# Pace of the second MoE's first weights, precedence of its first input sums, and place of the rests' last output products

## The chip, the core and the metric

The kernel runs on one core of one Trainium2 chip. The metric is device time in microseconds, median of the runs. A profiled execution has a span (first to last instruction) and a time of its own, which is a little longer than the span.

## What is computed

Nyström attention, then a gated MLP (SiLU gate, called layer 1 here) and a second one (sigmoid gate, layer 2), on 4 batches of 576 tokens.

```python
A, Bm, C = sm(q, k_lm), sm(q_lm, k_lm), sm(q_lm, k)      # 32 landmarks
Z = pinv_by_6_iterations(Bm)
x = (A @ Z @ C @ v)                                      # (2304, 512)
g = x @ w_gate;  x = (g * sigmoid(g) * (x @ w_val)) @ w_out      # layer 1, d_ff 1536
gate = sigmoid(x @ w_gate2);  out = (gate * (x @ w_val2)) @ w_out2   # layer 2
```

## The kernel before

All matrices are split into a high and a low fp32r part, and a product is three matmuls (high·high, low·high, high·low). The MLP weights arrive as 64-bit floats. `convert` turns a raw tile into fp32 with two ScalarE instructions (L329, L332) and two VectorE instructions (L334, L338); `split` makes the high part by a ScalarE cast (L365) and the low part by a VectorE subtraction (L366).

**Layer 1** goes over six chunks `c` of 256 hidden columns and four batches `b`. A string of words sets the order: `U` makes the chunk's folded weights `uw`, `G` the gate and value products (`pg`, `pv`), the gate function on ScalarE (L528, tile `sg`), its product with the value on VectorE (L529, tile `h`) and the split of `h`; `O` makes the output products `po`, added to `acc` on VectorE (L583). So `G50` is chunk 5, batch 0. The first 64 tokens of each batch are gathered into a block of 256 tokens, the *rests*, which is batch number 4 in `O` words and in layer 2. Between the steps of a word, `emit` takes `nw` steps out of `wfill`, the list of weights that are still to be prepared. From the word after `G43` on, the first weights of layer 2 (`weights(1, 0)`) are in that list. Whatever is left when layer 2 begins is done at once by `need(1, 0, 3)` at L834.

**Layer 2** runs in two passes: `st` 1 for batches 0 and 1 and the rests, `st` 2 for batches 2 and 3. A pass treats its input as 2 x 2 blocks and makes seven block products instead of eight. `x_blocks` prepares it for each half `j` of the inner dimension: four sums `xs` (L615 to L618), and for seven blocks a high part in `AH` and a low part `xl` (L366). `pair_steps` issues the block products (`pg`, `pv` with the chunk and the product number in their names), `rest_steps` the rests' (`pgr`, `pvr`), and `o2_steps` the output products of the chunk before, added to `oacc` (L750) and, after the last chunk, written out by four DMAs a tile on SyncE's queue (L756). The argument `ths` of `o2_steps` is the order: 0 and 1 are the two batches of the pass (four tiles of 128 tokens each), 2 the rests (two tiles).

Buffers come from pools with a set number of slots. The two `oacc` tiles of the rests live in the pool `xs`, and so do the sums `xs` and some low parts `xl` of both passes: an `xl` of the second pass takes the slot of a rests' tile when that has been written out. PSUM has three slots for `gv`, two each for `o` and `a`, and one for `n`; every fourth gate or value product of layer 1, and the value of product 2 in layer 2, takes the slot `n`.

The instructions of an engine run in the order in which a scheduler put them, by the program's order and its priorities (`tc.high_priority(n)` moves work forward by `n`). Each engine and each DMA queue is in order.

Of the kernel before, what the change touches and what calls it, by code (L numbers as in the profile page):

```python
# [16 lines left out]
def nystrom_moe_kernel(tc, q, k, v, wg1, wv1, wo1, wg2, wv2, wo2, out):  # L17
# [11 lines left out]
    NFC = DFF // FC  # L29
# [4 lines left out]
    def pool(name, side=None, **kw):  # L34
        return tc.alloc_tile_pool(name=name, bufs=1, side=side, reuse_waits="tile", **kw)
# [10 lines left out]
    def ptile(shape, tag, name):  # L46
        return psum.tile(shape, F32, tag=tag, name=name, bufs=PB[tag])

    late = {}
# [14 lines left out]
    def mm(o, l, r, start=True, stop=True):  # L64
        return nc.tensor.matmul(o, l, r, start=start, stop=stop, skip_group_check=True)  # L65
# [27 lines left out]
    def step(fill, n=1):  # L93
        while n and fill:
            try:
                next(fill[0])
                n -= 1
            except StopIteration:
                fill.pop(0)
# [264 lines left out]
    def split(hi, lo, x):  # L364
        nc.scalar.copy(hi, x)  # L365
        nc.vector.tensor_tensor(lo, x, hi.bitcast(F32), op=ALU.subtract)  # L366
# [60 lines left out]
    def weights(layer, c):  # L427
        if layer == 0:
            W1[c] = w1p.tile([P, 4, 2, FC], F32, tag="w1", name=f"w1_{c}", bufs=2)
            wo_tile(layer, c)  # L430
            i0 = PIECES.index((layer, c, load_in, 0))
            for j in range(4):
                load_to(i0 + j + 3)
                yield from convert(loaded[i0 + j], W1[c][:, j])
        else:
            wo_tile(layer, c)
            for j in range(2):
                yield from in_weights(layer, c, j)
        ready.add((layer, c, 3))
        for j in range(2):  # L440
            yield from out_weights(layer, c, j)
        ready.add((layer, c, 5))
        load_to(PIECES.index((layer, c, load_out, 1)) + 4)
# [8 lines left out]
    def need(layer, c, part):  # L452
        while (layer, c, part) not in ready:
            step(wfill)
# [11 lines left out]
    def otag(layer, c):  # L466
        nps[0] += 1
        return "oa"[nps[0] % 2] if layer or c >= OA else "o"
# [4 lines left out]
    ACC = {}  # L473
# [68 lines left out]
    NR = S - MT  # L542
# [61 lines left out]
    def x_blocks(step_, x):  # L604


        hi = [AH[:, s, NR:] for s in range(16)]
        for j in range(2):
            def new(n, dt, home):
                pool_, bufs = (per, 16) if home == "CL" else (late["xs"], 8)  # L610
                return pool_.tile([P, MT], dt, tag=home, name=f"x{n}{step_}_{j}", bufs=bufs)

            a11, a12, a21, a22 = x[0][j], x[0][2 + j], x[1][j], x[1][2 + j]
            s1, s2, s3, s4 = (new(f"s{n}", F32, "xs") for n in range(1, 5))
            nc.vector.tensor_tensor(s1, a21, a22, op=ALU.add)  # L615
            nc.vector.tensor_tensor(s3, a11, a21, op=ALU.subtract)
            nc.vector.tensor_tensor(s2, s1, a11, op=ALU.subtract)
            nc.vector.tensor_tensor(s4, a12, s2, op=ALU.subtract)  # L618
            for n, at, src, home in ((1, 0, a11, "CL"), (2, 8, a12, "CL"), (4, 9, a22, "CL"), (5, 2, s1, "CL"),
                                     (6, 10, s2, "xs"), (7, 1, s3, "xs"), (3, 3, s4, "xs")):  # L620
                lo = new(f"l{n}", F32R, home)
                split(hi[at + 4 * j], lo, src)
                XB[n, j] = (hi[at + 4 * j], lo)
# [107 lines left out]
    def o2_steps(step_, c, ths):  # L731
        w = WO[step_, c]
        for th in ths:
            h = [H2[ft, th] for ft in range(2)]
            i = th + 2 * step_ - 2 if th < 2 else B
            for t in range(0, MT if i < B else NR * B, P):
                if c == 0:
                    OACC[i, t] = (per.tile([P, DM], F32, tag="CL", name=f"oacc{i}_{t}", bufs=16) if i < B else
                                  late["xs"].tile([P, DM], F32, tag="xs", name=f"oacc{i}_{t}", bufs=8))
                acc = OACC[i, t]  # L740
                ps = ptile([P, DM], otag(1, c), f"po2_{c}_{i}_{t}")
                n = 0
                for ft in range(2):
                    for a, x in TERMS:
                        mm(ps, h[ft][a][:, t:t + P], w[:, x, ft, :], start=(n == 0), stop=(n == 5))
                        n += 1
                if c == 0:
                    nc.scalar.copy(acc, ps)
                else:
                    nc.vector.tensor_tensor(acc, ps, acc, op=ALU.add)  # L750
                if c == NFC - 1:
                    rows = out.rearrange("(b t u) d -> b u t d", b=B, u=L)
                    for y in range(P // M):
                        bb, u = (i, (NR + t) // M + y) if i < B else ((t + M * y) // NR, (t + M * y) % NR // M)
                        eng = nc.scalar if y % 2 and step_ == 2 else nc.sync
                        eng.dma_start(rows[bb, u], acc[M * y:M * y + M, :])  # L756
                yield
# [19 lines left out]
    def emit(word, nw=1):  # L777
        gens = [iter(KINDS[t[0]](*map(int, t[1:]))) for t in word.split("+")]
        fill = word[0] in "UPGO"
        while gens:  # L780
            for g in list(gens):
                try:
                    next(g)
                except StopIteration:
                    gens.remove(g)
            if fill:
                step(wfill, nw)
# [18 lines left out]
    for word in words.split():  # L806
        kind, c, bs = word[0], int(word[1]), [int(b) for b in word[2:]]
        if kind == "G" and bs == [1] and c < NFC - 1:
            wfill.append(weights(0, c + 1))
        if kind == "O":  # L810
            need(0, c, 5)
        elif kind != "G":
            need(0, c + bs[-1] // B, 3)
        emit(word, 2)
        if word == f"G{NFC - 2}3":
            late["uw"].release()
            late["w2"] = pool("w2")
            late["x"] = pool("x")
            wfill.append(weights(1, 0))
    w1p.release()  # L820
    late["xs"] = pool("xs")
    x_blocks(1, [[ACC[b, dm][:, NR:] for dm in range(4)] for b in range(2)])

    def run(g, n=100, nw=2):
        for _ in range(n):
            try:
                next(g)
            except StopIteration:
                return
            step(wfill, nw)  # L830
# [11 lines left out]
    prev = None  # L842
    for st in (1, 2):
        for c in range(NFC):
            if st == 1 or c + 1 < NFC:
                wfill.append(weights(st, c + 1) if c + 1 < NFC else weights(2, 0))
            rest = rest_steps(c) if st == 1 else iter(())
            o2 = iter(())
            if prev:
                need(*prev, 5)  # L850
                o2 = o2_steps(*prev, (0, 1) if prev[0] == 2 else (0, 1, 2) if prev[1] == NFC - 1 else (2, 0, 1))
            if (st, c) == (1, NFC - 1):
                x2 = [[per.tile([P, MT], F32, tag="CL", name=f"x2{b}_{dm}", bufs=16) for dm in range(4)]
                      for b in range(2)]
                for dm in (0, 2, 1, 3):
                    for b in range(2):
                        nc.sync.dma_start(x2[b][dm], XP[b + 2, dm])
            if (st, c) == (2, 0):
                x_blocks(2, x2)
            run(o2, 10 if (st, c) == (2, 0) else 4 if st == 2 else 6)  # L860
            need(st, c, 3)
            if c < NFC - 1:
                run(rest)
            if prev:
                g2 = pair_steps(st, c)
                run(g2, 5)
            for n in (4, 2, 4):
                run(o2, 1)
                run(g2, n)
            run(o2)  # L870
            run(g2)
            run(rest)
            prev = (st, c)
# [39 lines left out]
```

## Time and profile before

| | |
|---|---|
| median of 3 runs | 884.43 us (882.47 to 886.38) |
| profiled execution, own time | 883.13 us |
| its span | 881.3 us |
| PE busy | 843.0 us, 96% of the span |
| VectorE (DVE) busy | 662.4 us, 75% |
| ScalarE (ACT) busy | 475.2 us, 54% |
| mean granted TensorE clock | 0.988 of full speed |

TensorE (PE) is busy nearly all the time, so what can be had lies in the few places where it stands still, and in the work that runs at the lower of its two clock levels (1.2 in place of 2.4 GHz) after it. Busy shares are read by stage: another engine may be full in a stage in which its average is low.

### The profile page before, as it was taken

How to read it: one execution, taken by the hardware profiler on the slowest of the kernel's cores; microseconds unless marked ns; L12 is line 12 of the kernel's file. 1: busy time of each engine (PE TensorE's matmuls, PEld its weight loads, DVE VectorE, ACT ScalarE, POOL GpSimd, SP SyncE). 2: the span in 40 equal slices, each digit the busy share in tenths (PEclk: the TensorE clock that was granted, in tenths of full speed). 3: DMA queues.
4: the chain of work that ended last, by engine and by line, in shares of the span. 5: the costliest groups of instructions: out<-in, count | busy, mean ns of one | idle time of the engine just before them, and what ended most of it. 6: DMA issues, size and time to landing. Idle time of an engine off the chain costs nothing.

```text
span 881.3 us, 15891 instructions
## 1 busy us (share of the span) xinstructions
PE 843.0 (96%) x6172; PEld 698.7 (79%) x6172; DVE 662.4 (75%) x1295; ACT 475.2 (54%) x967; POOL 57.7 (7%) x90
## 2 busy tenths in 40 slices
PE   5698999999999999997999999999999899999998
PEld 4386778888889888887878888888888778888886
DVE  4989776776886776689698667879789965687655
ACT  5787556355653443357347655555646465455431
POOL 4634330000000000000000000000000000000000
PEclk9899999999999999998999999999999989999999
DMA  8876211032430211036204315344255442242003
GB/s 267 211 218 201 81 56 29 3 96 69 124 96 18 68 60 49 1 143 208 79 34 158 120 45 195 97 143 167 97 179 170 123 134 89 95 120 71 1 25 96
DMA packets 41483, 93.31 MB, mean 106 GB/s; under 512 B 5824, under 2 KB 8896, under 8 KB 41408
## 3 DMA queue, kind: packets, MB, share of 16 engines
q1 hardware_dynamic: 40640, 91.25, 33.2%
q10 hardware_dynamic: 768, 1.05, 0.5%
q8 instruction: 48, 0.79, 0.4%
q14 instruction: 27, 0.22, 0.1%
HBM read 72.88 MB, written 19.40 MB: 105 GB/s over the span
## 4 chain that ended last, share of the span: by engine, by line
PE 83%; DVE 9%; ACT 3%; DMA 3%; issue 1%; SPq 1%; POOL 0%; ACTq 0%; DVEq 0%; POOLq 0%
PE po L65 31%; PE pg L65 20%; PE pv L65 20%; PE pu L65 2%; DMA raw<-in_moe_w_val_dram 2%; PE pgr L65 2%; PE pvr L65 2%; PE tp L148 1%; PE nw L65 1%; DVE cv L334 1%; PE cs L65 1%; DVE xl L366 1%; PE as L65 1%; DVE acc L583 1%; ACT cv L329 1%
## 5 line engine op out<-in xcount | busy, mean ns | idle before, releaser
L65 PE MATMUL po<-wo,h 128*128 128x512 f32 x432 | 109.5, 390 | 0.0
L65 PE MATMUL po<-h,wo 128*128 128x512 f32 (+1 forms) x480 | 105.4, 374 | 0.3 <-DVE uw L366 0.2
L65 PEld LDWEIGHTS po<-h,wo 128*128 128x128 f32 x480 | 83.4, 190 | 27.3 <-issue 7.5
L65 PE MATMUL pv<-AH,uw 128*128 128x288 f32 x552 | 93.3, 300 | 5.7 <-ACT sg L528 5.2
L65 PE MATMUL pg<-AH,uw 128*128 128x288 f32 x552 | 95.6, 300 | 1.3 <-ACT uw L365 1.0
L65 PEld LDWEIGHTS po<-wo,h 128*128 128x128 f32 x432 | 80.7, 188 | 17.6
L65 PEld LDWEIGHTS pv<-AH,uw 128*128 128x128 f32 x552 | 80.2, 191 | 10.1 <-ACT sg L528 6.1
L65 PEld LDWEIGHTS pg<-AH,uw 128*128 128x128 f32 x552 | 80.8, 189 | 6.5 <-issue 2.5
L750 DVE TENSOR_TENSOR oacc<-po,oacc 128x512 f32<-128x512 f32 x90 | 60.2, 685 | 31.5 <-PE po L65 31.4
L329 ACT ACTIVATE cv<-raw 128x512 f32<-128x512 f32 x84 | 56.7, 676 | 35.5 <-DVE st L338 8.8
L65 PE MATMUL pg<-AH,wt 128*128 128x512 f32 x192 | 60.8, 398 | 2.0 <-DVE wt L425 2.0
L65 PE MATMUL pv<-AH,wt 128*128 128x512 f32 x192 | 60.5, 396 | 0.0
L65 PE MATMUL po<-hh,wo 128*128 128x288 f32 x256 | 58.9, 310 | 0.0
L334 DVE SCALAR_TENSOR_TENSOR cv<-cv,cv 128x512 uint32<-128x512 uint32 x84 | 57.8, 692 | 0.8 <-ACT cv L332 0.8
L332 ACT ACTIVATE cv<-raw 128x512 uint32<-128x512 uint32 x84 | 56.1, 672 | 4.2 <-DVE wo L366 4.1
L583 DVE TENSOR_TENSOR acc<-po,acc 128x512 f32<-128x512 f32 x64 | 43.6, 687 | 18.2 <-PE po L65 17.9
L528 ACT ACTIVATE sg<-pg 128x288 f32<-128x288 f32 x64 | 26.0, 406 | 45.7 <-PE pg L65 45.6
L365 ACT CAST h<-h 128x288 fp32r<-128x288 f32 x64 | 27.5, 433 | 34.1 <-DVE h L529 34.1
L65 PEld LDWEIGHTS po<-hh,wo 128*128 128x128 f32 x256 | 41.6, 188 | 4.8 <-issue 2.4
L65 PEld LDWEIGHTS pg<-AH,wt 128*128 128x128 f32 x192 | 36.6, 191 | 10.3 <-DVE wt L425 2.4
L65 PE MATMUL pv<-AH,wk 128*128 128x512 f32 x144 | 44.3, 389 | 0.0
L65 PE MATMUL pg<-AH,wk 128*128 128x512 f32 x144 | 44.1, 390 | 0.0
(196 smaller groups left out, 1741.0 us busy)
## 6 DMA issues: line engine op xcount, KB each, us to landing
raw<-in_moe_w_out_dram SPq DMA_DIRECT2D x36, 512.0 KB, 4.3
raw<-in_moe_w_gate_dram SPq DMA_DIRECT2D x48, 128.0 KB, 2.9
raw<-in_moe_w_val_dram SPq DMA_DIRECT2D x48, 128.0 KB, 2.9
raw<-in_moe_w_gate_dram SPq DMA_DIRECT2D x24, 256.0 KB, 3.0
raw<-in_moe_w_val_dram SPq DMA_DIRECT2D x24, 256.0 KB, 3.7
wkd<-st SPq DMA_DIRECT2D x24, 256.0 KB, 3.2
wtd<-tf SPq DMA_DIRECT2D x12, 512.0 KB, 3.5
st<-wkd SPq DMA_DIRECT2D x24, 256.0 KB, 2.9
```

The lines of the kernel that those rows point to most:

```text
L65: return nc.tensor.matmul(o, l, r, start=start, stop=stop, skip_group_check=True)
L148: nc.tensor.transpose(ps[:, j], flat(src[:, 2 * u:2 * u + 2]), ident)
L329: nc.scalar.activation(t0, hiw.bitcast(F32), AF.Copy, scale=2.0 ** -112)
L332: nc.scalar.activation(u1, low, AF.Copy, scale=0.875 * 2.0 ** -29, bias=0.49)
L334: nc.vector.scalar_tensor_tensor(u1, u0, 3, u1, op0=ALU.logical_shift_left, op1=ALU.bitwise_or)
L365: nc.scalar.copy(hi, x)
L366: nc.vector.tensor_tensor(lo, x, hi.bitcast(F32), op=ALU.subtract)
L528: nc.scalar.activation(sg, pss[0], AF.Silu)
L583: nc.vector.tensor_tensor(sl, ps, sl, op=ALU.add)
L750: nc.vector.tensor_tensor(acc, ps, acc, op=ALU.add)
```

## The change

Three edits, none of which adds or removes an instruction.

```diff
@@ layer 1's words
-        emit(word, 2)
+        emit(word, 1 if late.get("w2") else 2)
         if word == f"G{NFC - 2}3":
             late["uw"].release()
             late["w2"] = pool("w2")
...
     late["xs"] = pool("xs")
-    x_blocks(1, [[ACC[b, dm][:, NR:] for dm in range(4)] for b in range(2)])
+    with tc.high_priority(300):
+        x_blocks(1, [[ACC[b, dm][:, NR:] for dm in range(4)] for b in range(2)])
...
-                o2 = o2_steps(*prev, (0, 1) if prev[0] == 2 else (0, 1, 2) if prev[1] == NFC - 1 else (2, 0, 1))
+                o2 = o2_steps(*prev, (0, 1) if prev[0] == 2 else (0, 2, 1) if prev[1] == NFC - 1 else (2, 0, 1))
```

The first takes one step of layer 2's first weights where two were taken, in the words after `G43`. The second gives the sums and splits of the first pass precedence. The third puts the rests' last output products between those of batch 0 and batch 1 when the second pass begins.

**First place: ScalarE at `G50`.** Before, between the first two gates (`sg_5_0`; `cv`, `wk`, `wo` and `wt` are weights):

```order
L424 CAST wt_0_0_5546<-tf_0_0_5496 128x1024
L365 CAST wk_0_01_5577<-st_0_1_5557 128x512
L329 ACTIVATE cv_5625<-raw 128x512
L332 ACTIVATE cv_5626<-raw 128x512
L528 ACTIVATE sg_5_0_5680<-pg_5_0_5666 128x288
L365 CAST wk_0_11_5602<-st_0_1_5557 128x512
L329 ACTIVATE cv_5660<-raw 128x512
L332 ACTIVATE cv_5661<-raw 128x512
L365 CAST wo_0_5494<-cv_5626 128x512
L329 ACTIVATE cv_6354<-raw 128x512
L332 ACTIVATE cv_6355<-raw 128x512
L528 ACTIVATE sg_5_0_5705<-pg_5_0_5691 128x288
```

And now, at the same place:

```order
L329 ACTIVATE cv_5670<-raw 128x512
L332 ACTIVATE cv_5671<-raw 128x512
L424 CAST wt_0_0_5586<-tf_0_0_5496 128x1024
L528 ACTIVATE sg_5_0_5637<-pg_5_0_5623 128x288
L528 ACTIVATE sg_5_0_5662<-pg_5_0_5648 128x288
L365 CAST h<-h_5_0_5638 128x288
L365 CAST wk_0_01_5645<-st_0_1_5601 128x512
L528 ACTIVATE sg_5_0_5688<-pg_5_0_5674 128x288
L365 CAST h<-h_5_0_5663 128x288
L329 ACTIVATE cv_5748<-raw 128x512
L528 ACTIVATE sg_5_0_5709<-pg_5_0_5695 128x288
```

Six weight instructions stood between the first gate and the second; now the two are neighbours, and the weights stand between the gates of `G50`, `G51` and `G52`. VectorE's weights move in the same way.

**Second place: VectorE and TensorE at the start of layer 2.** `h_5_3_6127` is the last of layer 1's four products of `G53`, `xs` and `xl` the first pass's sums and low parts. VectorE, as a piece of the difference:

```order
 L366 TENSOR_TENSOR h<-h_5_3_6107,h 128x288
-L529 TENSOR_TENSOR h_5_3_6127<-sg_5_3_6126,pv_5_3_6119 128x288
 L615 TENSOR_TENSOR xs_0_6136<-acc_0_2339,acc_2_2357 128x512
-L366 TENSOR_TENSOR h<-h_5_3_6127,h 128x288
 L616 TENSOR_TENSOR xs_0_6138<-acc_0_1131,acc_0_2339 128x512
 L617 TENSOR_TENSOR xs_0_6137<-xs_0_6136,acc_0_1131 128x512
...
 L366 TENSOR_TENSOR xl_1_6188<-xs_1_6167,AH 128x512
 L366 TENSOR_TENSOR xl_1_6191<-xs_1_6168,AH 128x512
+L529 TENSOR_TENSOR h_5_3_6127<-sg_5_3_6126,pv_5_3_6119 128x288
+L366 TENSOR_TENSOR h<-h_5_3_6127,h 128x288
```

`h_5_3_6127` and its low part stood before and behind the first of the sums; now all 19 instructions of `x_blocks` from L615 `xs_0_6136` to L366 `xl_1_6191` go first. TensorE after the change, from the first value product of layer 2 on:

```order
L65 MATMUL pv_1_0_1_6212<-AH,wk_0_01_5645 128x512 x2
L65 MATMUL po_5_3_6236<-h,wo_5_5090 128x512 x3
L65 MATMUL po_5_3_6246<-h,wo_5_5090 128x512 x3
L65 MATMUL po_5_3_6256<-h,wo_5_5090 128x512 x3
L65 MATMUL po_5_3_6266<-h,wo_5_5090 128x512 x3
L65 MATMUL pg_1_0_1_6198<-xl_1_6173,wk_0_01_5645 128x512
L65 MATMUL pv_1_0_1_6212<-xl_1_6173,wk_0_01_5645 128x512
L65 MATMUL pg_1_0_2_6205<-xl_1_6176,wk_0_11_5718 128x512
L65 MATMUL pv_1_0_2_6219<-AH,wk_0_10_5554 128x512 x2
L65 MATMUL pv_1_0_2_6219<-xl_0_6147,wk_0_10_5554 128x512
L65 MATMUL pv_1_0_2_6219<-AH,wk_0_11_5718 128x512 x2
L65 MATMUL pv_1_0_2_6219<-xl_1_6176,wk_0_11_5718 128x512
```

Before, the five matmuls of `pv_1_0_2` that need no `xl_1` stood directly behind `pv_1_0_1`, and the products `po_5_3` came whole; now `po_5_3` comes in halves, and `pv_1_0_2` comes behind the first halves. It takes the PSUM slot `n` of `pv_5_3_6119`, which is free when the moved L529 has read it.

**Third place: SyncE's queue at the start of the second pass.** `oacc_0_6556` and `oacc_128_6573` are the rests' tiles, the other `oacc` those of batches 0 and 1.

```order
 L756 DMA out_dram<-oacc_384_6637 32x512 x4
+L756 DMA out_dram<-oacc_0_6556 32x512 x4
+L756 DMA out_dram<-oacc_128_6573 32x512 x4
 L756 DMA out_dram<-oacc_0_6800 32x512 x4
 L756 DMA out_dram<-oacc_128_6860 32x512 x4
 L756 DMA out_dram<-oacc_256_6887 32x512 x4
-L756 DMA out_dram<-oacc_384_6927 32x512 x4
-L756 DMA out_dram<-oacc_0_6556 32x512 x4
-L756 DMA out_dram<-oacc_128_6573 32x512 x4
+L756 DMA out_dram<-oacc_384_6927 32x512 x3
+L414 DMA tf_1_1_8475<-wtd_1_6518 128x1024
+L756 DMA out_dram<-oacc_384_6927 32x512
```

The rests' output DMAs move from the 33rd to 40th place among the forty to the 17th to 24th, and a weight load (`tf_1_1`) now stands ahead of the last output DMA and of the weight loads behind it. On VectorE the rests' additions (L750) move forward by the same four tiles.

## Rows read from the trace of the kernel before

**Rows 1.** Page, parts 1 and 4: busy us by engine; chain that ended last

```profile
PE 843.0 (96%) x6172; PEld 698.7 (79%) x6172; DVE 662.4 (75%) x1295; ACT 475.2 (54%) x967; POOL 57.7 (7%) x90
...
PE 83%; DVE 9%; ACT 3%; DMA 3%; issue 1%; SPq 1%; POOL 0%; ACTq 0%; DVEq 0%; POOLq 0%
```

**Rows 2.** Stretches: width, then busy us of each engine, clock, DMA

```profile
core 0: us, PE busy (x) PEld busy (x) DVE busy (x) ACT busy (x) POOL busy (x), PEclk, DMA share, GB/s
...
396.50:401.70 5.20, 0.04 (x6) 0.00 (x0) 5.15 (x17) 2.18 (x5) 0.00 (x0) 0.91 0.57 204
401.70:408.30 6.60, 6.56 (x25) 6.14 (x26) 6.10 (x13) 6.10 (x13) 0.00 (x0) 0.56 0.64 191
408.30:423.00 14.70, 14.55 (x95) 11.96 (x93) 12.74 (x25) 11.07 (x22) 0.00 (x0) 1.00 0.60 201
...
457.40:459.40 2.00, 0.01 (x1) 0.00 (x0) 2.00 (x4) 0.00 (x0) 0.00 (x0) 1.00 0.00 0
...
702.50:705.50 3.00, 0.03 (x1) 0.03 (x1) 1.38 (x4) 0.67 (x1) 0.00 (x0) 0.84 0.58 145
705.50:711.90 6.40, 6.40 (x16) 4.78 (x17) 2.02 (x3) 1.87 (x4) 0.00 (x0) 0.54 0.73 234
...
381.70:433.95 52.25, 46.73 (x295) 39.51 (x281) 44.85 (x95) 33.28 (x66) 0.00 (x0) 0.93 0.47 162
444.30:467.76 23.46, 20.55 (x111) 16.90 (x109) 22.73 (x43) 12.29 (x23) 0.00 (x0) 1.00 0.12 45
```

**Rows 3.** Chain that ended last, 400 to 440 us: start, us, what

```profile
400.08 0.61 DVE wo L366
400.72 0.67 ACT cv L332
401.39 0.31 ACT sg L528
...
401.74 1.81 PE pv L65 x6
403.54 1.44 PE pg L65 x6
...
406.42 1.97 PE po L65 x6
...
432.43 5.71 PE po L65 x24
438.13 0.80 PE pg L65 x6
```

**Rows 4.** VectorE in order of time at the start of layer 2

```profile
443.97 0.46 DVE L366 TENSOR_TENSOR h<-h,h 128x288 fp32r<-128x288 f32 x1 [0.50 <-ACT h L365]
444.60 0.46 DVE L529 TENSOR_TENSOR h<-sg,pv 128x288 f32<-128x288 f32 x1 [0.17 <-PE pv L65]
...
448.35 1.89 DVE L366 TENSOR_TENSOR xl<-xs,AH 128x512 fp32r<-128x512 f32 x3
```

**Rows 5.** TensorE in order of time, same place: start, us, instructions

```profile
448.87 4.01 PE L65 MATMUL po<-h,wo 128*128 128x512 f32 x17
...
459.40 0.50 PE L65 MATMUL pg<-AH,wt 128*128 128x512 f32 x1 [1.99 <-DVE wt L425]
```

**Rows 6.** Chain that ended last at 703 us

```profile
702.92 1.72 DMA out_dram<-oacc
```

**Rows 7.** VectorE in order of time, 689 to 707 us

```profile
689.23 0.69 DVE L750 TENSOR_TENSOR oacc<-po,oacc 128x512 f32<-128x512 f32 x1
...
701.85 1.29 DVE L338 SCALAR_TENSOR_TENSOR cv<-cv,cv 128x512 uint32<-128x512 uint32 x2
704.72 2.15 DVE L366 TENSOR_TENSOR xl<-xs,AH 128x512 fp32r<-128x512 f32 x3 [1.59 <-DMA out_dram<-oacc]
```

**Rows 8.** SyncE's queue in order of time, 660 to 722 us

```profile
685.10 20.14 SPq L756 DMA_DIRECT2D out_dram<-oacc  x40
...
719.90 0.32 SPq L414 DMA_DIRECT2D tf<-wtd  x1
```

## Prediction

> **What bounds the kernel now.** I read the chain that ended last first: 83% of it is TensorE's work [rows 1]. Only a place where TensorE stands still, or runs at its lower clock level, can give time back, so next I looked in the order of time for its gaps near the three edits, and then asked which engine ends each of them.
>
> The first gap lies in `G50`. From 396.50 to 401.70 TensorE is busy for 0.04 us, while VectorE is busy for 5.15 of the 5.20 us [rows 2]. The chain there is weights: VectorE's `wo` subtraction releases a ScalarE conversion (L332), behind it in ScalarE's queue stands the second gate `sg`, and only that releases TensorE at 401.74 [rows 3]. Then the granted clock is 0.56 over 6.60 us [rows 2]: six matmuls take 1.81, 1.44, 1.44 where 0.80 is usual, and six `po` take 1.97 against a quarter of 5.71, which is 1.43 [rows 3]. That is 1.01 + 0.64 + 0.64 + 0.54 = 2.83 us lost to the clock, and 5.2 + 2.8 = 8.0 us for the whole place.
>
> The second place is the start of layer 2. Of 23.46 us TensorE is busy for 20.55, VectorE for 22.73 [rows 2]: 2.9 us of gaps, the largest 1.99, a wait for the low part of `wt` (L425) [rows 5]. The clock stays at 1.00 through it [rows 2].
>
> The third is the start of the second pass. TensorE stands still for 2.97 of the 3.00 us from 702.50, and the clock falls: 16 matmuls take 6.40 us [rows 2], where 17 of the same size take 4.01 at the full level, 0.23 each [rows 5]. 16 x 0.23 is 3.7, so the clock costs 2.7 us there. VectorE had stood 1.59 us waiting for an output DMA of a rests' tile, before the first of three `xl` [rows 7], and that DMA took 1.72 us to land [rows 6].
>
> **Edit 1, half the pace.** The second gate now follows the first on ScalarE, and TensorE's gap at 396.5 goes with its reason. What is late next? The weights are not fewer. Both orders have the same 95 instructions on VectorE from the last product of `G43` to the last low part of `G52`, and they were busy for 44.85 us between 381.70 and 433.95 [rows 2]. If VectorE now runs them without a pause it ends at 426.55, 7.4 us earlier. TensorE's work in the same stretch, 46.73 us less 2.83 of slow clock, is 43.9 and would end at 425.6. So VectorE, not TensorE, sets the gain: the output products after `G52` need its last low part, and TensorE should meet short waits ahead of `O51` and `O52` (I count 0.5 and 1.0 us by going through the gates one by one), not another long gap. The upper bound is 8.0. The lower bound is VectorE at the share of its nearest neighbour stretch with gates and weights mixed, 12.74 of 14.70 us, 87% [rows 2]: 44.85 / 0.87 is 51.6, and the gain 0.7. I take 7.0, near the upper end, since VectorE held 99% in the gap itself, where it had work queued as it now has throughout. The stores and loads of weights on SyncE's queue come later with their conversions, and the loads for the next chunk land behind the gates of `G50` and `G51`, so I cost that at nothing; if one came late, its L329 would stand on ScalarE in front of a gate, a gap of the kind of 396.5 again, at most its 8.0.
>
> **Edit 2, precedence.** It moves VectorE's last product of `G53` (L529, 444.60 in the trace [rows 4]) and its low part behind all 19 instructions of `x_blocks`. The three merged `xl` take 1.89 us [rows 4] with 0.69 for one [rows 7], so the next starts each 0.60 us. The preceding low part starts at 443.97 [rows 4], which leaves VectorE free for the sums at 444.34; 19 x 0.60 later it is 455.7, and L529 ends at 456.2, some 11 us later than before. Two things wait for it on TensorE. `pv_1_0_2` takes the PSUM slot that L529 reads, and the second halves of `po_5_3` need the last `h`. Queued ahead of them is too little: 15 block matmuls and 12 of `po` at 0.23, 6.2 us from 444.3, so to 450.5, and then three single ones that follow the `xl` (0.7 us). The gap, in three parts, is 456.25 - 450.5 - 0.7 = 5.05 us, against 2.9 before. The wait for `wt` goes, as L425 is now done before TensorE comes to it. The net is +2.15; the bounds are +1.0, if the short restarts of before go too (I reach that by laying the later rows end to end), and +4.1, if the wait for `wt` (1.99) remains beside it.
>
> The clock is the second part. A gap of 1.99 us left it alone, gaps of 2.97 and 5.2 did not [rows 2]. Here 5.05 us of idling are broken by 0.7 us of work, and the last piece alone is over 3 us. I take a fall, at 2.3 us: less than the 2.7 and 2.8 of the other two, because part of the slow time can lie in the broken gap. Bounds: 0 and 2.8. The Trainium skill (TensorE: Matmul & The Clock Gate, A second HAM failure mode: psum-queue depth-cycling) says that short idling between groups of matmuls is enough to make the clock swing; it speaks against this edit. By it the sum is as below; by the row of the 1.99 us gap alone it would be 2.3 us lower. The trace has no broken gap of this length.
>
> **Edit 3, the rests in the middle.** SyncE issues forty output DMAs in 20.14 us from 685.10 [rows 8], 0.50 each, in order. The rests' first tile moves from 33rd to 17th place, so its fourth DMA is issued by 685.1 + 20 x 0.50 = 695.2 and lands by 697. Its addition now stands where L750 ran at 689.23 [rows 7], early enough. VectorE comes to the `xl` when its two L338 are through, 701.85 + 1.29 = 703.1 [rows 7]. So the wait for the DMA goes, with six microseconds to spare, but VectorE's own queue still holds TensorE to about 703.9. The gap shrinks from 2.97 to 1.4 us, a gain of 1.6. A gap of 1.4 is shorter than the 1.99 that left the clock alone, so I take the 2.7 of the slow stretch as won too: 4.3. The bounds are 1.6 and 4.3. One thing is moved past: the load of `tf_1_1`, which was issued at 719.90 [rows 8] when its tile was free, now stands ahead of the last output DMA and four weight loads. They will come some 10 us later than before; their readers belong to the chunk after, so I cost this at nothing, with up to 1 us if ScalarE meets one of them late.
>
> **Sum.** Against the profiled execution's own 883.13: 883.13 - 7.0 + 2.15 + 2.3 - 4.3 = 876.3. That execution lies 1.3 us under the median of the runs, 884.43, inside their spread of 3.9. I predict 876.5.
>
> **The rivals.**
>
> *The precedence costs nothing* (chance 0.15). `x_blocks` finishes earlier in relation to TensorE, if VectorE enters it ahead of TensorE, and the broken gap stays short of a fall. For it: VectorE has no weights left in `G53`. Against: L529 is tied to 19 rows of 0.60 whatever comes before, and the sums cannot begin before the low part at 443.97. Without the clock's 2.3 and half the gap: 872 to 874.
>
> *VectorE holds TensorE all the way* (0.13). Edit 1 gains 3 in place of 7, because each gate's way from ScalarE to VectorE and back leaves gaps of 0.50, as in rows 4, which now also delay weights. It gives 880 to 882.
>
> *The clock falls anyway in the second pass* (0.09): the 1.4 us gap meets other short waits. Then only 1.6 is won, and the time is 879.
>
> *Slower* (0.08). The weights, spread among the gates, leave VectorE with as many pauses as before. Its share over the whole stretch was 44.85 of 52.25, 86% [rows 2]. At that share edit 1 gives nothing and the sum is 883.3, where it decides; at 75%, its mean over the kernel [rows 1], the stretch takes 59.8 us, 7.5 more, `x_blocks` starts late as well, and the time is 890. For it: each conversion goes through two in-order engines. Against: 99% in the gap.
>
> **How the numbers follow.** The forecast has 0.55, with 874 to 879 as its own range. About 0.5% (4.4 us) is what a measurement of this kernel can tell from no change. Below 880.0 lie the forecast, the first rival and the third: 0.79. Within 0.5% lie the second and the smaller part of the last: 0.13 + 0.03. Slower: 0.05. The range 871 to 881.5 leaves out the last rival, and some of the first with all bounds in its favour.
>
> **What would show it.** Step 1: no gap of TensorE at `G50`, granted clock 1.0 there, VectorE over 95% busy to the end of `G52`. Step 2: a new gap behind the first halves of `po_5_3`, in pieces, ended by VectorE's `h` (L529), with a clock near 0.55 behind it. Step 3: no wait of `xl` for `out_dram`, a gap of some 1.4 us, and full clock behind it. I am wrong if the second gate of `G51` or `G52` shows a long wait, if the broken gap is under 3 us, or if the clock falls in the second pass.

## The result and the profile after

The change makes the kernel faster: 875.53 us (874.01 to 877.95, 4 runs) against 884.75 us for the kernel before beside it (882.47 to 886.38, 4 runs), a ratio of 0.990 with a 95% interval of 0.9868 to 0.9933. On another chip, in the experiments below, the whole change took 875.5 against 882.9 us, 0.9912 (0.9896 to 0.9928). 876.5 had been forecast, by a sum of -6.85 us. The total fits; its three terms do not fit equally well.

The page of the kernel after, in the parts that answer to [rows 1]: busy time by engine, then the granted clock in 40 slices, then the chain that ended last.

```profile
PE 843.9 (96%) x6172; PEld 699.2 (80%) x6172; DVE 661.9 (76%) x1295; ACT 475.7 (54%) x967; POOL 57.6 (7%) x90
...
PEclk9789999999999999999999999999999999999999
...
PE 88%; DVE 6%; ACT 3%; issue 2%; DMA 1%; SPq 0%; DVEq 0%; ACTq 0%
```

Nothing in the amount of work has changed. TensorE's share of the chain has risen from 83% to 88%, and VectorE's and DMA's have fallen from 9% and 3% to 6% and 1%: TensorE waits less often. The PEclk row shows no slice under 9 behind the third. It also shows a 7 in the second slice, in a part of the program that is the same in both kernels. This execution (own time 877.95, span 876.2) comes to the first place that the change touches 4.4 us later than the profile of before. A second profile of the same kernel, told below, comes to it only 0.5 us later (375.62 against 375.09 us), so that those 4.4 us do not belong to the change, and everything that follows is measured from the place of an edit to the next.

The stretches of the kernel after, as in [rows 2], one for each place: where the gap of `G50` was, from the first gate product of `G43` to that of `G53`, from there to the second block of the rests' gate products, the new gap in that stretch and the work behind it, and the start of the second pass with the work behind it.

```profile
core 0: us, PE busy (x) PEld busy (x) DVE busy (x) ACT busy (x) POOL busy (x), PEclk, DMA share, GB/s
396.50:412.00 15.50, 15.50 (x108) 13.38 (x108) 15.50 (x35) 11.11 (x24) 0.00 (x0) 1.00 0.41 148
...
379.48:434.14 54.66, 54.37 (x361) 46.81 (x360) 49.23 (x105) 34.90 (x73) 0.00 (x0) 1.00 0.48 164
...
434.14:466.80 32.66, 28.23 (x157) 24.19 (x156) 27.92 (x52) 15.29 (x30) 0.00 (x0) 0.95 0.13 49
...
446.80:452.46 5.66, 1.23 (x3) 0.48 (x3) 5.61 (x10) 1.71 (x4) 0.00 (x0) 1.00 0.00 0
452.46:459.00 6.54, 6.54 (x25) 5.43 (x26) 4.45 (x7) 4.35 (x6) 0.00 (x0) 0.74 0.11 40
...
701.66:705.00 3.34, 2.03 (x8) 1.32 (x9) 2.64 (x5) 1.75 (x3) 0.00 (x0) 1.00 0.50 122
705.00:712.62 7.62, 7.62 (x35) 6.10 (x33) 4.67 (x8) 5.08 (x9) 0.00 (x0) 1.00 0.00 0
```

The same two stretches in the kernel before:

```profile
375.09:437.97 62.88, 57.35 (x361) 49.26 (x360) 50.82 (x106) 35.91 (x73) 0.00 (x0) 0.95 0.42 143
...
437.97:467.76 29.79, 26.88 (x158) 23.23 (x156) 27.28 (x52) 14.93 (x30) 0.00 (x0) 1.00 0.15 54
```

From `G43` to `G53` 62.88 us have become 54.66: 5.24 us less idling and 2.98 us less busy time, which is the clock, 0.95 before and 1.00 now. Where TensorE had stood still for 5.2 us, it is busy for 15.50 of 15.50, and so is VectorE. From `G53` to the rests 29.79 have become 32.66: idling rises from 2.91 to 4.43, and 1.35 us are lost to a clock that is 0.74 behind the gap.

TensorE of the kernel after in order of time, only the instructions that waited; at a row's end in brackets the idle time ahead and what ended it:

```profile
428.57 5.74 PE L65 MATMUL po<-h,wo 128*128 128x512 f32 x24 [0.29 <-ACT h L365]
...
447.88 0.50 PE L65 MATMUL pg<-xl,wk 128*128 128x512 f32 x1 [1.09 <-DVE xl L366]
448.22 0.40 PE L65 MATMUL pv<-xl,wk 128*128 128x512 f32 x1
449.09 0.50 PE L65 MATMUL pg<-xl,wk 128*128 128x512 f32 x1 [0.47 <-DVE xl L366]
452.46 1.22 PE L65 MATMUL pv<-AH,wk 128*128 128x512 f32 x2 [2.87 <-DVE h L529]
...
702.97 0.50 PE L65 MATMUL pg<-xl,wt 128*128 128x512 f32 x1 [1.31 <-DVE xl L366]
```

These are the waits that the three edits leave. The 1.99 us for `wt` of [rows 5] is gone. In its place stands a gap in three parts, 1.09 + 0.47 + 2.87 = 4.43 us, and its last part is ended by the `h` of `G53` that the precedence has moved. The 2.97 us at the start of the second pass are 1.31.

VectorE of the kernel after, at the same places:

```profile
386.10 0.46 DVE L529 TENSOR_TENSOR h<-sg,pv 128x288 f32<-128x288 f32 x1 [0.18 <-PE pv L65]
...
429.89 0.45 DVE L366 TENSOR_TENSOR h<-h,h 128x288 fp32r<-128x288 f32 x1
...
440.14 0.46 DVE L366 TENSOR_TENSOR h<-h,h 128x288 fp32r<-128x288 f32 x1 [0.50 <-ACT h L365]
440.52 0.68 DVE L615 TENSOR_TENSOR xs<-acc,acc 128x512 f32<-128x512 f32 x1
...
451.95 0.46 DVE L529 TENSOR_TENSOR h<-sg,pv 128x288 f32<-128x288 f32 x1
...
701.02 1.29 DVE L338 SCALAR_TENSOR_TENSOR cv<-cv,cv 128x512 uint32<-128x512 uint32 x2
702.22 2.15 DVE L366 TENSOR_TENSOR xl<-xs,AH 128x512 fp32r<-128x512 f32 x3
```

From the last product of `G43` (386.10) to the last low part of `G52` (ends at 430.34) VectorE takes 44.24 us, and is busy for 43.73 of them; its busy time in the same work before was 44.85 [rows 2]. The sums begin 6.4 us behind the first gate product of `G53`, and the moved L529 comes 17.8 us behind it. In the second pass the three `xl` follow the two L338 at once; the 1.59 us wait for the output DMA [rows 7] is gone.

### The profile page after: what moved, and what is told of

It reads as the page before. It is cut to its first block, busy times and chain, and to the rows that moved or that the text cites. A ratio compares the mean times of both kernels' runs of the same rounds, so it can differ in the third digit from the quotient of the medians.

```text
span 876.2 us, 15889 instructions
## 1 busy us (share of the span) xinstructions
PE 843.9 (96%) x6172; PEld 699.2 (80%) x6172; DVE 661.9 (76%) x1295; ACT 475.7 (54%) x967; POOL 57.6 (7%) x90
## 4 chain that ended last, share of the span: by engine, by line
PE 88%; DVE 6%; ACT 3%; issue 2%; DMA 1%; SPq 0%; DVEq 0%; ACTq 0%
PE po L65 34%; PE pv L65 21%; PE pg L65 21%; PE pu L65 3%; PE pgr L65 2%; PE pvr L65 2%; PE tp L148 2%; PE nw L65 1%; PE cs L65 1%; PE as L65 1%; PE et L198 1%; DVE xl L366 1%; DVE cv L334 1%; DMA raw<-in_moe_w_val_dram 1%; DVE cv L338 1%
## 5 line engine op out<-in xcount | busy, mean ns | idle before, releaser
L750 DVE TENSOR_TENSOR oacc<-po,oacc 128x512 f32<-128x512 f32 x90 | 60.3, 686 | 31.6 <-PE po L65 31.4
L65 PEld LDWEIGHTS pv<-AH,wt 128*128 128x128 f32 x192 | 36.0, 188 | 8.4
```

## The experiments

Each kernel is timed beside the kernel before on its chip, and the ratio to it carries a 95% interval. The first four ran on one chip (before: 883.13 us, 17 runs), the other four on another (882.9 us, 9 runs).

**One edit at a time.** Each of the first three kernels has one of the three pieces of the change's diff and nothing else.

```diff
-        emit(word, 2)
+        emit(word, 1 if late.get("w2") else 2)
```

> Edit 1 alone. Theory (three separate terms, read from the trace after the change): the gap in G50 goes and nothing else changes. From the first gate product of G43 to that of G53 it takes 54.7 us (63.0 before), from there to the second block of rests' products in layer 2 29.6 us as before, the second pass is as before; 884.75 - 8.4 = 876.4 us. Rival (backlog): the weights that edit 1 delays reach VectorE late and are what layer 2's start paid for; then that stretch takes 32.6 us here too, and the time is 879.3 us.

Measured: 875.87 us, 0.9918 (0.9903 to 0.9933).

```diff
-    x_blocks(1, [[ACC[b, dm][:, NR:] for dm in range(4)] for b in range(2)])
+    with tc.high_priority(300):
+        x_blocks(1, [[ACC[b, dm][:, NR:] for dm in range(4)] for b in range(2)])
```

> Edit 2 alone. Theory: the gap behind the first halves of the chunk 5 output products appears with the precedence alone; from the first gate product of G53 to the second block of rests' products 32.6 us (29.6 before), 887.7 us in all. Rival (backlog): 29.6 us and 884.7 us, as precedence does no harm without delayed weights.

Measured: 887.1 us, 1.004 (1.0026 to 1.0053): slower by 0.4%.

```diff
-  (0, 1, 2) if prev[1] == NFC - 1
+  (0, 2, 1) if prev[1] == NFC - 1
```

> Edit 3 alone. Theory: VectorE's wait for the output DMA goes, the gap at the second pass falls from 3.0 to about 1.3 us and the clock stays up behind it: 4.2 us, 880.6 us in all. Rival (phase): the clock stayed up after the whole change only because the earlier edits shifted its timing; then the gap falls but the clock still goes down, 1.6 us, 883.1 us.

Measured: 880.03 us, 0.9968 (0.9956 to 0.9981).

**The change without the precedence**: the first and the third of these pieces.

> Edits 1 and 3 without the precedence. Theory: 8.4 + 4.2 us less than before, 872.2 us, about 3 us under the whole change, with no gap behind the first halves of the output products. Rival (backlog): no better than the whole change, 875.5 us, with the loss at layer 2's start still there.

Measured: 872.65 us, 0.9879 (0.9861 to 0.9897).

What follows: the two edits that gain do so alone and together, -7.3 and -3.1 us alone and -10.5 together. The precedence costs 4.0 us alone. The expected times were reckoned from 884.75 us, the kernel before on the first chip; here it took 883.13, so the differences are what can be compared:

| kernel | theory, us | rival, us | measured, us (95% interval) |
|---|---|---|---|
| half pace alone | -8.4 | -5.5 | -7.3 (-8.6 to -5.9) |
| precedence alone | +3.0 | 0.0 | +4.0 (+2.3 to +4.7) |
| rests alone | -4.2 | -1.6 | -3.1 (-3.9 to -1.7) |
| half pace and rests | -12.6 | -9.2 | -10.5 (-12.3 to -9.1) |

For the first two the interval holds the theory and leaves out the rival. Where the rests are moved the times do not decide: both theories ask for 0.3 us more than the interval allows, one rival lies at its edge and the other inside it. There the traces decide. With the rests alone (first two rows) the gap is 1.31 us and the clock behind it 1.00, where the rival wanted a fall. With half pace and rests (last row) the longest wait at layer 2's start is that for `wt`, as before, and no gap in pieces is there:

```profile
705.44 0.50 PE L65 MATMUL pg<-xl,wt 128*128 128x512 f32 x1 [1.31 <-DVE xl L366]
...
706.00:712.00 6.00, 6.00 (x26) 4.62 (x26) 2.65 (x5) 3.51 (x7) 0.00 (x0) 1.00 0.13 33
...
452.84 0.50 PE L65 MATMUL pg<-AH,wt 128*128 128x512 f32 x1 [1.98 <-DVE wt L425]
```

The stretches show where each difference sits. The table gives, in us, the distances between four instructions on TensorE's timeline: the first gate product of `G43`, that of `G53`, the second block of the rests' gate products, and the output products ahead of chunk 1 in the second pass. From the last of these to the end of the span all of them take 163.5 to 163.7.

| kernel | `G43` to `G53` | to the rests | to the second pass |
|---|---|---|---|
| before | 62.88 | 29.79 | 249.89 |
| half pace alone | 54.67 | 31.29 | 248.58 |
| precedence alone | 63.24 | 33.82 | 249.59 |
| rests alone | 62.43 | 31.28 | 245.79 |
| half pace and rests | 54.67 | 31.29 | 245.77 |
| whole change, first profile | 54.66 | 32.66 | 245.82 |
| whole change, second profile | 54.62 | 33.90 | 245.86 |

Each edit moves one column. The half pace takes the first from 62.4 to 63.2 down to 54.6 to 54.7, and the rests take the third from 248.6 to 249.9 down to 245.8. The middle column is odd: the half pace and the rests leave its work alone, and yet it is 1.5 us longer with them than before. It counts in the times: added up over the three columns, the traces differ from that of before by -8.0 us (half pace), +4.1 (precedence), -3.1 (rests) and -10.8 (half pace and rests), near the timed -7.3, +4.0, -3.1 and -10.5. The rests alone gain 4.1 us in their own column and lose 1.5 in the middle one. Here is that place in the kernel before:

```profile
460.20 2.31 PE L65 MATMUL po<-h,wo 128*128 128x256 f32 x18
...
459.40:463.45 4.05, 4.05 (x28) 3.72 (x28) 3.95 (x8) 0.43 (x1) 0.00 (x0) 1.00 0.58 217
```

And with the half pace alone, with the same instructions behind the same wait; the last two rows are the start of its second pass:

```profile
451.59 0.50 PE L65 MATMUL pg<-AH,wt 128*128 128x512 f32 x1 [1.99 <-DVE wt L425]
...
452.39 3.47 PE L65 MATMUL po<-h,wo 128*128 128x256 f32 x18
...
451.59:457.15 5.56, 5.56 (x28) 5.13 (x28) 4.04 (x8) 0.44 (x1) 0.00 (x0) 0.69 0.51 189
...
699.00 1.52 PE L65 MATMUL pg<-xl,wt 128*128 128x512 f32 x2 [2.78 <-DVE xl L366]
...
699.00:705.40 6.40, 6.40 (x21) 4.85 (x22) 2.05 (x3) 2.55 (x5) 0.00 (x0) 0.74 0.75 259
```

The wait is 1.99 us in both. Before, 28 matmuls behind it take 4.05 us at a clock of 1.00; here the same 28 take 5.56 at 0.69. So a 2 us gap can lower the clock, and in the profile of before it happened not to. In the second pass it is the other way round: there the profile of before shows the long fall, 16 matmuls in 6.40 us at 0.54 [rows 2], while in this one 21 fit into the same time.

**The whole change again**, unaltered, beside the kernels below.

> The whole change once more, so that the precedence's price on top of the other two edits is read against one baseline. Theory (the precedence always costs 1.5 us of idling, 4.43 against 2.91, and a clock fall that partly replaces one that the wait for the low part of wt brings anyway): 0.9879 of the two other edits plus about 3 us, so a ratio near 0.991. Rival (the single edits add up, -7.3 + 4.0 - 3.1): -6.4 us, a ratio of 0.9927.

Measured: 875.5 us, 0.9912 (0.9896 to 0.9928). Its stretch from `G53` to the rests, and the work behind its gap:

```profile
430.24:464.16 33.92, 29.49 (x158) 25.07 (x156) 28.04 (x52) 15.30 (x30) 0.00 (x0) 0.90 0.13 47
...
448.56:456.45 7.89, 7.89 (x25) 6.40 (x26) 5.48 (x9) 4.33 (x6) 0.00 (x0) 0.62 0.14 51
```

The idling is 33.92 - 29.49 = 4.43 us again, but 25 matmuls need 7.89 us at 0.62 where the first profile has 25 in 6.54 at 0.74. The ratio is 0.0033 above that of the half pace with the rests, some 2.9 us; the two intervals touch, so this price is known to a microsecond or two only. The sum of the single edits, -6.4, has 0.9927, which the interval still holds.

**A ninth slot in place of edit 3.** Half the pace, the rests' products left where they were, and one slot more in the pool that the `xl` share with the rests' tiles.

```diff
-                 pool_, bufs = (per, 16) if home == "CL" else (late["xs"], 8)
+                 pool_, bufs = (per, 16) if home == "CL" else (late["xs"], 9)
...
-  name=f"oacc{i}_{t}", bufs=8))
+  name=f"oacc{i}_{t}", bufs=9))
...
-        emit(word, 2)
+        emit(word, 1 if late.get("w2") else 2)
```

> Half the pace, the rests' output products left at the end, and a ninth slot for the tiles of the sums and of the outputs, so that no conversion of the second pass waits for an output transfer. Theory (edit 3 gained by taking that transfer wait away, and with it the clock fall behind the gap): the 3.0 us gap at the start of the second pass shrinks to 1.4 us or less at full clock, and the time falls by 3 to 5.6 us from the half pace alone, 0.9918, to 0.9855 to 0.988. Rival (edit 3 gained by the place of the products on TensorE, not by the wait): no change, 0.992.

Measured: 870.32 us, 0.9856 (0.9838 to 0.9873). The start of its second pass:

```profile
687.00:702.00 15.00, 15.00 (x67) 12.19 (x66) 13.91 (x24) 9.43 (x17) 0.00 (x0) 1.00 0.36 89
```

TensorE has no gap at all there, and the clock holds. With the outputs in the old order, it was the transfer wait that cost the time, not the place of the products on TensorE. The gain over the half pace alone is 0.0062, 5.5 us, against edit 3's 0.0039; the two kernels ran on different chips and their intervals overlap, so that the times alone leave it open which is better. In the trace the scheduler has put the `xl` ahead of the weight conversions as well, and the 1.31 us for which VectorE's own queue still holds TensorE after edit 3 are gone too.

**The low part of `wt` earlier.** The kernel of the ninth slot, and

```diff
-    t_split(1, 0, 1)
+    with tc.high_priority(100):
+        t_split(1, 0, 1)
```

> As the kernel before it, with the low part of the first wt of layer 2 (L425) put into the middle of VectorE's block of sums and conversions. Theory (the 1.99 us wait is one late instruction, and the clock fall behind it, 1.5 us in three of four traces, hangs on that wait): 2 to 3.5 us less than the kernel without it. Rival (VectorE, busy for 27.3 of the 29.8 us, bounds this stretch): the wait goes to the conversions behind L425, and the time stays within 0.5 us.

Measured: 868.77 us, 0.984 (0.9825 to 0.9855), the fastest of all, though its interval overlaps that of the kernel without this piece. The stretch from `G53` to the rests in that kernel:

```profile
429.99:461.28 31.29, 28.37 (x158) 24.63 (x156) 27.74 (x52) 14.94 (x30) 0.00 (x0) 0.95 0.14 51
```

And with the earlier `wt`, its waits beside it:

```profile
429.88:459.80 29.92, 27.60 (x158) 23.18 (x156) 27.64 (x52) 14.93 (x30) 0.00 (x0) 1.00 0.15 54
...
450.31 0.50 PE L65 MATMUL pg<-xl,wt 128*128 128x512 f32 x1 [0.34 <-DVE xl L366]
...
452.11 3.37 PE L65 MATMUL po<-h,wo 128*128 128x256 f32 x24 [1.07 <-DVE acc L583]
```

Both theories hold in part; the difference of the medians, 1.55 us, lies in the range of neither. The wait for `wt` is gone, but 1.07 us for an addition to `acc` and 0.34 for an `xl` stand in its place, since VectorE is busy for 27.64 of 29.92 us: idling falls by 0.6 us only. The clock holds at 1.00, and the stretch is 1.37 us shorter. It is still no shorter than in the kernel before, where 29.79 us held the wait for `wt` and a clock that had not fallen.

**The gates of `G53` ahead of the sums.** The whole change, and

```diff
-        emit(word, 1 if late.get("w2") else 2)
+        with tc.high_priority(400) if word == "G53" else nullcontext():
+            emit(word, 1 if late.get("w2") else 2)
```

> The whole change, with the gate instructions of G53 given a still higher precedence than the sums. Theory (what the precedence costs is the last h of G53 queued behind the sums): the 2.87 us wait for h is gone or under 0.5 us, the clock holds, and the time is 3 to 4.5 us under the whole change, near 0.986. Rival (the sums, later by the gate instructions ahead of them, hold TensorE by as much): the idling stays at about 4.4 us in other pieces, and the time is that of the whole change, 0.991.

Measured: 874.56 us, 0.9904 (0.9889 to 0.9919), not to be told from the whole change on that chip. TensorE's waits:

```profile
442.25 0.50 PE L65 MATMUL pg<-xl,wk 128*128 128x512 f32 x1 [1.57 <-DVE xl L366]
...
443.42 0.73 PE L65 MATMUL pg<-AH,wt 128*128 128x512 f32 x2 [0.44 <-ACT c1g L672]
...
448.25 9.91 PE L65 MATMUL po<-h,wo 128*128 128x512 f32 x46 [2.25 <-DVE acc L583]
...
448.25:456.00 7.75, 7.75 (x30) 6.39 (x31) 5.98 (x9) 0.00 (x0) 0.00 (x0) 0.78 0.57 214
```

The wait for `h` is gone, as it should be, and 1.57 + 0.44 + 2.25 = 4.26 us of others have come. The clock falls behind them as well, to 0.78 (last row), where the theory had it hold. The rival is right: in each order of VectorE's work tried so far, TensorE waits for what goes last in this stretch.

## Why the prediction was right

**Edit 1, -7.0 forecast: right in mechanism, too small by about 1 us in its stretch.** The stretch is 8.2 us shorter (62.4 to 63.2 before, 54.7 after), against an upper bound of 8.0; the timed gain alone is 7.3. The gap of `G50` is gone and the clock is 1.00, as step 1 said. VectorE runs on almost without a pause, 44.24 us where 44.85 had been taken, and busy for 99% of them. The step that failed is the one behind it, that the output products should meet short waits of 0.5 and 1.0 us ahead of `O51` and `O52`. There is one, of 0.29 us. TensorE began `O52` at 428.57, 1.77 us before VectorE was through with its last low part at 430.34: the 24 products need the four parts of `h` one after the other, so the last one may come late. The rows of before had shown as much: there `O52` began at 432.43 [rows 3], 1.52 us before VectorE was through at 433.95 [rows 2]. "VectorE, not TensorE, sets the gain" is wrong by that much; TensorE, busy for 54.37 of 54.66, sets it.

The timed gain is smaller than that of the stretch. One trace of each kernel does not settle why. In the traces two other stretches change with it and nearly cancel: the clock fall behind the wait for `wt` costs 1.5 us that before did not pay, and the fall at the start of the second pass is 1.3 us cheaper.

**Edit 2, +4.45 forecast: right in place and sign, 0.5 us too large alone and 1.5 to 2 us beside the other edits.** L529 was expected some 18.2 us behind the first gate product of `G53` (456.2 less 437.97) and ended 18.3 behind it (452.41 less 434.14); the broken gap, 5.05 forecast, is 4.43; the clock falls behind it. The net idling is +1.52 where +2.15 stood. The clock term has the larger error, and not because the fall was shorter: it costs 1.35, 2.51 and 2.61 us in three traces, against 2.3 forecast (busy time of 28.23, 29.39 and 29.49 us less 26.88). What failed is the rule that was drawn from one row, "A gap of 1.99 us left it alone". Five traces have that gap, of 1.98 to 2.01 us, and in four of them, all but that of before, the stretch is 31.28 or 31.29 us long in place of 29.79: 1.5 us of clock. The precedence takes that fall away along with the wait for `wt`, and only the difference of the two falls is its price in clock. Means over the traces are 33.46 us with it and 30.99 without, +2.5 us; timed, it costs 4.0 us alone and some 2.9 beside the other two.

The Trainium skill (TensorE: Matmul & The Clock Gate, A second HAM failure mode: psum-queue depth-cycling) tells of a kernel in which frequent short idling between groups of matmuls made the clock swing. The traces agree with it in kind, though here it is one gap, whole or in pieces, and not frequent idling: 0.74 and 0.62 behind a gap in pieces, 0.69 behind one of 1.99 us. The rule by the single row, which the prediction set against it, is the one that fell.

**Edit 3, -4.3 forecast: right in mechanism, 1 us too large in the time.** The wait for the transfer is gone, the gap is 1.31 where 1.4 was forecast, and the clock is 1.00 behind it. The idling term, -1.6, is measured as 1.66. The clock term was sized by the fall in the one profile of before, 2.7 us; the same place costs 1.3 us less with the half pace alone. The stretch gains 2.8 to 4.1 us by which trace it is read against, and the timed gain is 3.1 alone and 3.2 beside the half pace. In the trace of edit 3 alone its own stretch gains the 4.1; what the sum did not count is the 1.5 us that the fall behind the wait for `wt` takes back earlier. The load of `tf_1_1`, moved ahead of the last output DMA, cost nothing that shows: the four traces in the table with the rests in the middle agree within 0.1 us in the third column.

**The rivals.** That the precedence costs nothing, and that VectorE holds TensorE all the way, are excluded by the kernels with one edit alone. The clock did not fall in the second pass in any of the five traces with the third edit, and "slower" needed VectorE to pause as often as before, which it did not. That the total came so near is in part luck, since errors of either sign met: in the traces one more microsecond from edit 1, in the times 1.5 less lost to edit 2 and one less from edit 3.

Still open is what decides whether a 2 us gap lowers the clock: TensorE's instructions and waits around it are the same in the traces where it does and in the one where it does not. Nor is it settled that the precedence costs more alone (4.0) than on top (2.9); the intervals allow that it doesn't. Trace against trace it costs 4.0 us alone (33.82 against 29.79) and 1.4 or 2.6 on top (32.66 or 33.90 against 31.29), because the trace of before has no fall at the wait for `wt` and that of the half pace with the rests has one. Whether these single traces are typical of the timed runs is not shown.

## What to carry to other kernels

Where two engines take turns, slow down the work that has time: with half the weights per step VectorE did the same work almost without a pause between the gates, and a 5.2 us gap and its clock fall vanished. Before one instruction is put ahead of others on an engine that is over 90% busy in its stage, ask which one is then last, and who waits for that: here three orders of VectorE's work made TensorE wait for `wt`, for `h` or for `acc`, and moving a single late instruction was the one that may have gained, 1.4 us in its stretch, over half of it because no clock fall followed. Price a clock fall from more than one trace: the same gap had it or not.

## What was not expected of the hardware

The same wait of 1.98 to 2.01 us, with the same instructions around it, left TensorE's clock at 1.00 in one trace (28 matmuls in 4.05 us) and was followed by 0.69 in another (5.56 us); in four of five traces the clock fell. A gap of 2.97 us was followed by 16 matmuls in 6.40 us, one of 2.78 us at the same place by 21 in the same time. In the unchanged early part one profile of the changed kernel lost 3.9 us against the other (379.48 against 375.62 us to the first gate product of `G43`).
